# V and ones as weights from batch 2 on, with all attention steps at half slots: sparse attention beside a bilinear FFN

## Chip, cores, metric

One core of a Trainium2 chip. The metric is the device time of one execution in microseconds.

## The reference

```python
# q, k, v: (8, 8, 576, 64) f32, drawn * 0.1
scores = q @ k.T / 8                      # per batch and head, 576 x 576
local   = (0 <= i - j) & (i - j < 32)     # heads 0 to 3
strided = (0 <= i - j) & (j % 32 == i % 32)   # heads 4 to 7
attn = softmax(where(mask, scores, -1e9)); x = attn @ v
x -> (4608 tokens, 512 channels)
out = ((x @ w_a) * (x @ w_b)) @ w_out     # 512 -> 1536 -> 512
```

## The kernel before

The FFN runs over nine tiles of 512 tokens. A tile has 16 slots: 12 a/b slots (two groups of four matmuls, 1.73 us together) and four y slots (12 matmuls, 2.59 us). Attention steps of the next batch are put between the slots, since a tile needs the tokens of up to two batches. A batch has 8 S steps (scores, exp, mask), 8 V steps (probabilities times V, with a column of ones that gives the sums, then a reciprocal and a multiplication) and 4 X steps: TensorE (PE) transposes that bring the normalised output, tokens on partitions, to the channels-on-partitions form that the FFN reads, and a ScalarE copy. From batch 2 on, q and k are transposed by VectorE in 32x32 blocks ("D steps") and then moved to their places (`kT`, `qz`) by transfers that SyncE issues. The code is cut to the parts that matter.

```python
VW = 80
...
def step_D(b, z, nm, part):                   # z: 0 local heads, 1 strided
    nc.vector.transpose(t..., src...)         # 32x32 blocks
    if last:                                  # of k, or of q
        for nm, c in {"k": (("k", 0),), "q": (("q", 0), ("k", 1), ("q", 1))}[nm]:
            ...  nc.sync.dma_start(out=qz_buf[b % 2][j][z][...], in_=t[...])
...
def V_p(b, u):                                # from batch 2 on
    o = psum4["o"].tile([128, 2, 512], F32, tag="o", name="o")     # one buffer, two banks
    ...
    nc.tensor.matmul(of[:, j, i, :65], lhsT=p[:M, j, i*n:i*n+128], rhs=vt[..., 0:65], ...)
def V_r(b, u): nc.vector.reciprocal(rc, sums)
def V_n(b, u): nc.vector.tensor_mul(xn[...], o, rc broadcast)
def X_p(b, c): ... nc.tensor.transpose(tv[:, g, :], xn[:, g], ident)
def X_e(b, c): nc.scalar.copy(xT[:, c, S*b:S*(b+1)], tp)
...
open_psum(ctx, mm=3, tp=1, o=1)               # and "st", one buffer of two banks for scores
...
gs = {2: (13, 13, 14, 14, 15, 15, 16, 16, 17, 17), ...}    # slots of the ten D steps
for i, (fn, t, j) in enumerate(slots):
    fn(t, j, ...)                             # the FFN's work of the slot
    for f in at.get(i, ()): f()               # loads, D steps
    run(...)                                  # attention steps, whole slots
```

The softmax here doesn't subtract the row's maximum and nothing guards it: scores larger than these inputs give would overflow.

Of the kernel before, what the change touches and what calls it, by code (L numbers as in the profile page):

```python
# [7 lines left out]
F32 = mybir.dt.float32  # L8
BF16 = mybir.dt.bfloat16
I16 = mybir.dt.int16  # L10
ALU = mybir.AluOpType
ACT = mybir.ActivationFunctionType
ENG = mybir.EngineType

FIRST_D = 2
# [6 lines left out]
LW = 96  # L22
PAD = 32
PW = 344
VW = 80
WCH = (0, 2, 5, 8, 10, 12)


# [1 line left out]
def kernel(  # L30
# [66 lines left out]
    def consts(i):  # L97
# [7 lines left out]
        if i == 0:  # L105
            nc.vector.memset(vl_buf[0][:PAD, 0, 0:D], 0.0)

    spare = qz_buf[0][0][0][:, 0]

    def zero_qz(i, eng, parts=((0, 0), (0, 1), (1, 0), (1, 1))):  # L110
# [56 lines left out]
    def load_qk(b, strided, heads=range(HL), names="kq"):  # L167
        for nm in names:
            src = {"k": k, "q": q}[nm]
            if b < FIRST_D:  # L170
                n, R, h0 = (NP, RS, HL) if strided else (96, RL, 0)
                if (b, nm, strided) not in nats:
                    nats[b, nm, strided] = nat.tile([n, HL, R, D], BF16, tag=f"{nm}{R}", name=f"{nm}{R}", bufs=2)
                t = nats[b, nm, strided]
                hs = slice(heads[0], heads[-1] + 1)
                nc.gpsimd.dma_start(out=t[:, hs], in_=src[b, h0:h0 + HL].rearrange("h (p r) d -> p h r d", r=R)[:, hs])  # L176
            elif strided:

                t = nat_s[nm]
                n = 32 if b == FIRST_D else YS  # L180
                for h in heads:
                    nc.gpsimd.dma_start(  # L182
                        out=t[32 * h:32 * h + n],
                        in_=bass.AP(tensor=src.tensor, offset=(b * H + HL + h) * S * D,
                                    ap=[[RS * D, n], [YS * RS * D, 3], [1, RS * D]]))
            else:
                if 0 in heads:
                    nats[b, nm, strided] = nat.tile([128, NY, D], BF16, tag=f"{nm}l", name=f"{nm}l")
                t = nats[b, nm, strided]
                for h in heads:  # L190
                    nc.gpsimd.dma_start(out=t[32 * h:32 * h + 32],  # L191
                                        in_=src[b, h].rearrange("(i y) d -> y i d", y=32))
            nats[b, nm, strided] = t
# [122 lines left out]
    def unit(u):  # L316

        c, half = u // 2, u % 2
        return (c, half, 128, LW, 3) if c < 2 else (c, half, NP, NP, 4)
# [44 lines left out]
    def V_p(b, u):  # L364
        c, half, M, n, G = unit(u)
        p = ps.pop((b, u))
        if b == 0:

            o = psum4["o"].tile([128, 512], F32, tag="o", name="o")
            if c < 2:  # L370
                of = o[:, :2 * G * (D + 1)].rearrange("p (j g e) -> p j g e", j=2, e=D + 1)
                sm = of[:, :, :, D:]
            else:
                of = o.rearrange("p (j g e) -> p j g e", j=2, e=D)
                sm = psum4["sum"].tile([128, 2, 4, 1], F32, tag="sum", name="sum")
        else:
            o = psum4["o"].tile([128, 2, 512], F32, tag="o", name="o")
            of = o[:, :, :G * (D + 1)].rearrange("p j (g e) -> p j g e", e=D + 1)
            sm = of[:, :, :, D:]
        for i in range(G):  # L380
            for j in range(2):
                if c < 2:
                    vt = vl_buf[b % 2][:, (2 * c + j) * 6 + 3 * half + i, 0:D + 1]
                elif b == 0:
                    r = 2 * i + j
                    vt = nats[0, "v", c - 2][:NP, half, r * D:(r + 1) * D]
                elif b < FIRST_D:
                    vt = vs_buf[b % 2][:, 2 * (c - 2) + half, 2 * i + j, 0:D + 1]
                else:
                    vt = vs_buf[b % 2][:, 2 * (c - 2) + j, 4 * half + i, 0:D + 1]  # L390
                w = vt.shape[1]
                pt = p[:M, j, i * n:i * n + 128]
                nc.tensor.matmul(of[:, j, i, :w], lhsT=pt, rhs=vt, start=True, stop=True)  # L393
                if b == 0 and c >= 2:
                    nc.tensor.matmul(sm[:, j, i], lhsT=pt, rhs=vl_buf[0][:M, 0, D:D + 1], start=True, stop=True)
        held[b, "o", u] = of[:n, :, :, :D], sm[:n]
# [7 lines left out]
    def V_n(b, u):  # L404
        c, half, M, n, G = unit(u)
        ov, _ = held.pop((b, "o", u))
        rc = held.pop((b, "rc", u))
        if (b, c // 2) not in xn:
            xn[b, c // 2] = sb.tile([n, S // n, 4, D], BF16, tag=f"xn{n}", name=f"xn{n}", bufs=1)
        x = xn[b, c // 2][:, :, 2 * (c % 2):2 * (c % 2) + 2, :]  # L410
        if c < 2 or b >= FIRST_D:
            dst = x[:, G * half:G * half + G].rearrange("p g j d -> p j g d")
        else:
            dst = x[:, :, half, :].rearrange("p (g j) d -> p j g d", j=2)
        nc.vector.tensor_mul(dst, ov, rc[:n, :, :G].unsqueeze(3).to_broadcast([n, 2, G, D]))  # L415

    def step_V(b, u):
        V_p(b, u)
        V_r(b, u)
        V_n(b, u)  # L420

    def X_p(b, c):
        x = xn[b, c // 2][:, :, 2 * (c % 2):2 * (c % 2) + 2, :]
# [22 lines left out]
    def step_X(b, c):  # L446
# [12 lines left out]
        F1b F1c""".split()  # L459


    SEQ_T = {4: "Tk2", 5: "Tk3", 6: "Tq2", 7: "S4 Tq3", 8: "V4 S5", 9: "V5 S6 Tk0", 10: "V6 S7 Tq0",
             11: "V7 S0 X2", 11.5: "Tk1 S1", 12: "Tq1", 12.5: "X3 S2 V0", 13: "S3 V1", 13.5: "V2", 14: "V3 X0", 14.5: "X1"}
    DENSE = (("S0",), ("S1",), ("V0", "S2"), ("V1", "S3"), ("V2", "X0", "S4"), ("V3", "S5"), ("V4", "X1", "S6"),
             ("V5", "S7"), ("V6", "X2"), ("V7",), ("X3",))
    SEQ = (("S0",), ("S1",), ("V0",), ("S2",), ("V1",), ("S3", "X0"), ("V2",), ("S4",), ("V3",), ("S5", "X1"),
           ("V4",), ("S6",), ("V5",), ("S7", "X2"), ("V6",), ("V7",), ("X3",))
    FN = {"Tk": step_Tk, "Tq": step_Tq, "S": step_S, "V": step_V, "X": step_X}

    def run(b, slot):  # L470
        for s in slot:
            FN[s[:-1]](b, int(s[-1]))
# [1 line left out]

    pfs = {}

    def ab_mm(t, f, ab, kks):
        for w, ps_ in zip((wa_sb, wb_sb), ab):
            for kk in kks:
                nc.tensor.matmul(ps_, lhsT=w[:, kk, 128 * f:128 * (f + 1)], rhs=xT[:, kk, TTOK * t:TTOK * (t + 1)],  # L480
                                 start=(kk == 0), stop=(kk == KD - 1))

    def ffn_ab(t, f, ab=None):
        if f == 0:
            pfs[t] = fsb.tile([128, FD, TTOK], BF16, tag="pf", name="pf", bufs=1)
        pf = pfs[t]
        if ab is None:
            ab = [psum4["mm"].tile([128, TTOK], F32, tag="mm", name="mm") for _ in range(2)]
            ab_mm(t, f, ab, range(KD))
        a_sb = fsb.tile([128, TTOK], F32, tag="a_sb", name="a_sb")  # L490
        nc.scalar.copy(a_sb, ab[0])  # L491
        nc.vector.tensor_mul(pf[:, f, :], a_sb, ab[1])  # L492
        return pf[:1, f, :1]
# [21 lines left out]
    with tc.manual_schedule(engines={ENG.PE, ENG.SP, ENG.Pool, ENG.DVE, ENG.Activation}):  # L515
# [70 lines left out]
        slots = []  # L586
        for t in range(NT):
            slots += [(ffn_ab, t, f) for f in range(FD)] + [(ffn_y, t, j) for j in range(4)]
        todo = [(b, {2: 20}.get(b, 16 * (b - 1) - 2), list({2: DENSE}.get(b, SEQ)))
                for b in range(2, B)]  # L590
        at = {}

        def do(i, fn, *args):
            at.setdefault(i, []).append(lambda: fn(*args))

        for b in range(FIRST_D, B):
# [4 lines left out]
            else:  # L601
# [2 lines left out]
                    do(g0 + h + (6 if b == FIRST_D + 1 else 2), load_qk, b, True, (h,))  # L604
                    do(g0 + h + 10, load_vs, b, (h,))
                do(g0 + (10 if b == FIRST_D + 1 else 7), load_vl, b)
            gs = {2: (13, 13, 14, 14, 15, 15, 16, 16, 17, 17), 3: (8, 9, 10, 11, 12, 13, 14, 15, 16, 17)}.get(b) or (
                3, 5, 7, 9, 11, 12, 13, 14, 15, 17)
            for (z, nm, part), g in zip(((0, "k", 0), (0, "k", 1), (0, "q", 0), (0, "q", 1), (1, "k", 0), (1, "k", 1),
                                         (1, "k", 2), (1, "q", 0), (1, "q", 1), (1, "q", 2)), gs):  # L610
# [3 lines left out]
            do(6 + h, spread_vs, 1, h, nc.scalar.copy)  # L614
        do(1, zero_qz, 1, nc.vector, ((1, 1),))
        do(4, zero_qz, 1, nc.vector, ((1, 0),))
        for i, jz in ((2, (0, 0)), (3, (1, 0)), (12, (0, 1)), (12, (1, 1))):
            do(i, zero_qz, 0, nc.vector, (jz,))
        do(17, rezero, 1)
        for i, (fn, t, j) in enumerate(slots):  # L620
            if fn is ffn_y:
                done = fn(t, j, lambda: run(1, SEQ_T.get(i - 0.5, "").split()) if t == 0 else None)
            else:
                done = fn(t, j, first.get(j) if t == 0 else None)
            if i > 13 and i in at:

                nc.gpsimd.tensor_copy(pace, done)  # L627
            for f in at.get(i, ()):
                f()
            run(1, SEQ_T.get(i, "").split())  # L630
            for b, g0, seq in todo:
                if seq and i >= g0:
                    run(b, seq.pop(0))
# [1 line left out]
_INS = ['q', 'k', 'v', 'moe_w_a', 'moe_w_b', 'moe_w_out']  # L635
_OUTS = [((4608, 512), 'float32')]
# [25 lines left out]
```

## Time and profile before

| | before |
|---|---|
| time, median of 4 | 345.4 us (344.6 to 345.9) |
| TensorE busy | 98% |
| tile 0 / tile 1 / tiles 2 to 5 each / tile 6 / tile 7 | 42.83 / 36.61 / 35.90 / 35.40 / 31.08 us |
| gaps on TensorE in tiles 0 / 1 / 2 | 3.95 / 0.20 / none |

A tile is counted from the start of its first FFN matmul to that of the next tile. A gap is the distance between the starts of two neighbouring matmuls less the time in which the first streams its columns (columns / 2.4 GHz + 2.5 ns, which fits this trace: 216 ns for 512 columns, 43 for 96); this shows waits that the modelled ends of matmuls hide. The page and the views of this kernel are read in the prediction. One more view matters later, the one of the tile `qz01l`, a part of the transposed q, between 58 and 68 us: instruction, count, shortest, median and longest issue in ns, first and last start; then the time from issue to landing.

```profile
L299 SPq DMA_DIRECT2D qz01l<-tq x4: 539/590/1216, 60.3 to 66.8; - x4
...
DMA to landing us min/median/max: 2.6/4.1/6.4
```

Batch 2's first S step needs the first two of these and the first two of `qz00l`. The last of the four was issued at 62.18 us and landed 5.1 us later, at 67.3. TensorE came to the step at 70.35 us, with 3.1 us in hand:

```profile
70.35 0.21 PE L337 MATMUL st<-qz00l,kT0l 128*128 128x96 bf16 x1
```

### The profile page before, as it was taken

The numbers are of one execution on the slowest core, as the hardware profiler recorded it, in microseconds if no ns is written. First come the engines' busy times: TensorE is split into PE (matmuls) and PEld (weight loads), VectorE is DVE, ScalarE is ACT, GpSimd is POOL, SyncE is SP. The second block draws the span as 40 slices with busy tenths as digits, with TensorE's granted clock in tenths as the row PEclk, the third lists the DMA queues.
The fourth block names the chain that finished last, engine by engine and source line by source line (L and its number), as shares of the span: only waits on it lengthen the run. The fifth ranks groups of instructions, "written<-read, shape, count | busy, mean of one in ns | idle before, by whom it ended". The sixth has DMA issues, their size and how long they took to land.

```text
span 343.2 us, 7085 instructions
## 1 busy us (share of the span) xinstructions
PE 335.8 (98%) x2688; PEld 176.9 (52%) x2688; DVE 198.5 (58%) x400; ACT 152.8 (45%) x259; POOL 131.9 (38%) x243
## 2 busy tenths in 40 slices
PE   8999998999999999999999999999999999999995
PEld 6754554455555555555555555555555544444444
DVE  6865677669747764777377746774666323303331
ACT  5654864456255534544454435543454243223311
POOL 8944539596556334743375246533000000000000
PEclk9999999999999999999999999999999999999999
DMA  9999999996999879969996999788220110020002
GB/s 158 146 202 199 202 174 197 175 146 94 124 192 128 88 112 152 111 90 104 151 122 104 90 158 112 131 69 145 69 54 2 63 61 0 3 92 31 0 32 92
DMA packets 102243, 37.57 MB, mean 109 GB/s; under 512 B 77633, under 2 KB 97729, under 8 KB 102209
## 3 DMA queue, kind: packets, MB, share of 16 engines
q0 software_dynamic: 87760, 19.58, 62.3%
q1 hardware_dynamic: 14304, 17.47, 15.9%
q8 instruction: 21, 0.34, 0.4%
q14 instruction: 14, 0.11, 0.1%
q10 hardware_dynamic: 144, 0.07, 0.1%
HBM read 39.71 MB, written 9.44 MB: 143 GB/s over the span
## 4 chain that ended last, share of the span: by engine, by line
PE 81%; DMA 12%; POOL 4%; DVE 1%; issue 1%; ACT 0%; POOLq 0%; ACTq 0%
PE mm L480 48%; PE mm L502 24%; DMA vl<-in_v_dram 4%; PE st L337 4%; DMA k<-in_k_dram 3%; PE o L393 3%; DMA wa_sb<-in_moe_w_a_dram 3%; PE tp L428 2%; DMA out_dram<-y_sb 1%; DMA natk<-in_k_dram 1%; POOL q L176 1%; POOL vl L203 1%; POOL k L176 1%; POOL wa_sb L224 0%; POOL wb_sb L224 0%
## 5 line engine op out<-in xcount | busy, mean ns | idle before, releaser
L492 DVE TENSOR_TENSOR pf<-a_sb,mm 128x512 bf16<-128x512 f32 x106 | 72.8, 687 | 81.7 <-PE mm L480 77.9
L480 PE MATMUL mm<-xT,wa_sb 128*128 128x512 bf16 x424 | 108.9, 379 | 0.0
L480 PE MATMUL mm<-xT,wb_sb 128*128 128x512 bf16 x424 | 108.8, 379 | 0.0
L502 PE MATMUL mm<-wo_sb,pf 128*128 128x512 bf16 (+2 forms) x456 | 98.9, 368 | 0.0
L491 ACT COPY a_sb<-mm 128x512 f32<-128x512 f32 x106 | 62.0, 585 | 82.3 <-PE mm L480 80.8
L480 PEld LDWEIGHTS <-wb_sb 128*128 128x128 bf16 x432 | 42.2, 98 | 51.2 <-issue 0.4
L502 PEld LDWEIGHTS <-pf 128*128 128x128 bf16 x456 | 41.6, 98 | 42.6
L480 PEld LDWEIGHTS <-wa_sb 128*128 128x128 bf16 x432 | 37.4, 98 | 33.4
L345 ACT ACTIVATE p<-st 128x576 bf16<-128x576 f32 (+1 forms) x64 | 41.7, 651 | 25.9 <-PE st L337 25.8
L508 ACT COPY y_sb<-mm 128x512 f32<-128x512 f32 (+2 forms) x35 | 19.9, 570 | 70.6 <-PE mm L502 48.8
L415 DVE TENSOR_TENSOR xn<-o,rc 96x384 bf16<-96x384 f32 (+1 forms) x64 | 39.6, 620 | 2.1
L393 PEld LDWEIGHTS <-p 72*128 72x128 bf16 (+1 forms) x448 | 22.0, 97 | 16.5 <-DVE xn L415 3.5
L355 DVE TENSOR_TENSOR p<-p,mask_l 128x576 int16<-128x576 int16 x32 | 14.2, 443 | 24.6 <-ACT p L345 24.6
L627 POOL CAST pace<-pf 1x1 f32<-1x1 bf16 x51 | 8.9, 175 | 41.0 <-DVE pf L492 29.0
L215 POOL DMA_DIRECT2D vs<-in_v_dram x24 | 19.6, 817 | 10.6 <-issue 8.9
L444 ACT COPY xT<-tp 128x576 bf16<-128x576 bf16 x31 | 19.6, 634 | 3.3 <-PE tp L428 3.1
L401 DVE RECIPROCAL rc<-o 96x6 f32<-96x6 f32 (+1 forms) x60 | 11.3, 189 | 16.1 <-PE o L393 15.8
L191 POOL DMA_DIRECT2D kl<-in_k_dram x24 | 16.0, 665 | 7.4 <-issue 5.5
L191 POOL DMA_DIRECT2D ql<-in_q_dram x24 | 16.0, 666 | 5.8 <-DMA wo_sb<-in_moe_w_out_dram 3.7
L182 POOL DMA_DIRECT2D natk<-in_k_dram x24 | 14.6, 610 | 6.3 <-issue 6.3
L627 POOL COPY pace<-y_sb 1x1 f32<-1x1 f32 x22 | 3.8, 174 | 29.5 <-ACT y_sb L508 29.5
L182 POOL DMA_DIRECT2D natq<-in_q_dram x24 | 14.6, 608 | 0.0
(106 smaller groups left out, 283.1 us busy)
## 6 DMA issues: line engine op xcount, KB each, us to landing
out_dram<-y_sb SPq DMA_DIRECT2D x35, 256.0 KB, 2.1
vl<-in_v_dram POOLq DMA_DIRECT2D x7, 384.0 KB, 6.6
kl<-in_k_dram POOLq DMA_DIRECT2D x24, 72.0 KB, 3.1
ql<-in_q_dram POOLq DMA_DIRECT2D x24, 72.0 KB, 3.2
vs<-in_v_dram POOLq DMA_DIRECT2D x24, 72.0 KB, 3.7
wo_sb<-in_moe_w_out_dram POOLq DMA_DIRECT2D x4, 384.0 KB, 11.6
natk<-in_k_dram POOLq DMA_DIRECT2D x20, 72.0 KB, 3.1
natq<-in_q_dram POOLq DMA_DIRECT2D x20, 72.0 KB, 3.3
```

The lines of the kernel that those rows point to most:

```text
L182: nc.gpsimd.dma_start(out=t[32 * h:32 * h + n], in_=bass.AP(tensor=src.tensor, offset=(b * H + HL + h) * S * D, ap=[[RS * D, n], [YS * RS ...
L191: nc.gpsimd.dma_start(out=t[32 * h:32 * h + 32], in_=src[b, h].rearrange("(i y) d -> y i d", y=32))
L215: nc.gpsimd.dma_start(out=vs_buf[b % 2][:, h, :, 0:D], in_=v[b, HL + h].rearrange("(p r) d -> p r d", r=RS))
L345: nc.scalar.activation(p[:M, :, :W], st[:M, :, :W], ACT.Exp, scale=scale)
L393: nc.tensor.matmul(of[:, j, i, :w], lhsT=pt, rhs=vt, start=True, stop=True)
L415: nc.vector.tensor_mul(dst, ov, rc[:n, :, :G].unsqueeze(3).to_broadcast([n, 2, G, D]))
L444: nc.scalar.copy(dst, tv)
L480: nc.tensor.matmul(ps_, lhsT=w[:, kk, 128 * f:128 * (f + 1)], rhs=xT[:, kk, TTOK * t:TTOK * (t + 1)], start=(kk == 0), stop=(kk == KD - 1))
L491: nc.scalar.copy(a_sb, ab[0])
L492: nc.vector.tensor_mul(pf[:, f, :], a_sb, ab[1])
L502: nc.tensor.matmul(y, lhsT=pf[:, f, 128 * j:128 * (j + 1)], rhs=wo_sb[:, f, c0:c0 + n], start=(f == 0), stop=(f == FD - 1))
L508: (nc.scalar.copy if act else nc.vector.tensor_copy)(y_sb, y)
```

## The change

V with 64 columns of ones becomes the stationary operand and the probabilities the moving one. The output then has channels on partitions 0 to 63 and the sums, repeated, on 64 to 127. So no transpose is needed: ScalarE makes 1/sum as exp(-ln(sum)), VectorE multiplies twice and writes xT itself, for the strided heads with a stride. The price is 128-wide V buffers, filled with ones by GpSimd. All attention steps get positions in half slots, batch 2's D steps move (most of them one slot later), and the first group of a tile takes the channel that is made last at its end. The diff is shortened.

```diff
-VW = 80
+VW = 128
+def fill_v(t):
+    nc.gpsimd.memset(t[..., D:], 1.0)
...
+def step_VT(b, u):                                   # b >= 2
+    nc.tensor.matmul(o[:, j, i*n:(i+1)*n], lhsT=vt, rhs=p[:M, j, i*n:(i+1)*n], ...)
+    nc.scalar.activation(r, sums, ACT.Ln)            # o[64:], 64 x 576
+    nc.scalar.activation(r, r, ACT.Exp, scale=-1.0)
+    for j in range(2):
+        nc.vector.tensor_mul(xT[64*j:64*j+64, c, ...], o[:64, j, :W], r[:, j])
...
-SEQ_T, DENSE, SEQ = ...                              # whole slots, X steps in them
+STEPS = {1: {5: "Tk2", 5.5: "Tk3", ... 15: "X1"},
+         2: {20: "S0", 20.5: "S1", 21.5: "V0", 22: "S2", ... 30.5: "V7"}}
+LATER = {-2: "S0", -1: "S1", 0: "V0", 1: "S2", 2: "V1", ... 12: "V6", 13.5: "V7"}
...
+late = 1 if t == 1 else 3                            # first group of a tile
+ab_mm(t, f, ab, [kk for kk in range(KD) if kk != late], last=-1)
+ab_mm(t, f, ab, [late], first=-1, last=late)
...
-gs = {2: (13, 13, 14, 14, 15, 15, 16, 16, 17, 17), ...
+gs = {2: (14, 14, 14, 15, 16, 16, 17, 17, 18, 18), ...
+for i, t in ((0, vl_buf[0]), (0, vs_buf[0]), (18, vl_buf[1]), (19, vs_buf[1])):
+    do(i, fill_v, t)
```

Cut: one buffer in place of two for batch 0's and 1's q and k, one shared buffer for `xn` and `r`, other slots for some memsets, and the D steps now stand behind the attention steps of their slot in the queues.

More of the change, by code (lines that the diff above doesn't have):

```diff
@@ L106, in consts @@
             nc.vector.memset(vl_buf[0][:PAD, 0, 0:D], 0.0)
+    def fill_v(t):
+        nc.gpsimd.memset(t[:, :, :, D:] if len(t.shape) == 4 else t[:, :, D:], 1.0)
     spare = qz_buf[0][0][0][:, 0]
@@ L172, in load_qk @@
                 if (b, nm, strided) not in nats:
-                    nats[b, nm, strided] = nat.tile([n, HL, R, D], BF16, tag=f"{nm}{R}", name=f"{nm}{R}", bufs=2)
+                    nats[b, nm, strided] = nat.tile([n, HL, R, D], BF16, tag=f"{nm}{R}", name=f"{nm}{R}", bufs=1)
                 t = nats[b, nm, strided]
@@ L386, in V_p @@
                     vt = nats[0, "v", c - 2][:NP, half, r * D:(r + 1) * D]
-                elif b < FIRST_D:
+                else:
                     vt = vs_buf[b % 2][:, 2 * (c - 2) + half, 2 * i + j, 0:D + 1]
-                else:
-                    vt = vs_buf[b % 2][:, 2 * (c - 2) + j, 4 * half + i, 0:D + 1]
                 w = vt.shape[1]
@@ L408, in V_n @@
         if (b, c // 2) not in xn:
-            xn[b, c // 2] = sb.tile([n, S // n, 4, D], BF16, tag=f"xn{n}", name=f"xn{n}", bufs=1)
+            x = sb.tile([128, RS * 4 * D], BF16, tag="xr", name="xr", bufs=2)
+            xn[b, c // 2] = x[:n, :S // n * 4 * D].rearrange("p (g h d) -> p g h d", h=4, d=D)
         x = xn[b, c // 2][:, :, 2 * (c % 2):2 * (c % 2) + 2, :]
@@ L417, in step_V @@
     def step_V(b, u):
+        if b >= FIRST_D:
+            step_VT(b, u)
+            return
         V_p(b, u)
@@ L420, in step_V @@
         V_n(b, u)
+    def step_VT(b, u):
+        c, half, M, n, G = unit(u)
+        p = ps.pop((b, u))
+        o = psum4["o"].tile([128, 2, 512], F32, tag="o", name="o")
+        for i in range(G):
+            for j in range(2):
+                if c < 2:
+                    vt = vl_buf[b % 2][:, (2 * c + j) * 6 + 3 * half + i]
+                else:
+                    vt = vs_buf[b % 2][:, 2 * (c - 2) + j, 4 * half + i]
+                nc.tensor.matmul(o[:, j, i * n:(i + 1) * n], lhsT=vt, rhs=p[:M, j, i * n:(i + 1) * n], start=True, stop=True)
+        r = sb.tile([128, RS * 4 * D], BF16, tag="xr", name="xr", bufs=2)[:64, :4 * W].bitcast(F32)
+        r = r.rearrange("p (j w) -> p j w", j=2)
+        if c < 2:
+            sums = o[64:, :, :W]
+        else:
+            sums, r = (t.rearrange(e, p=NP) for t, e in ((o[64:, :, :W], "d j (g p) -> d j p g"), (r, "d j (p g) -> d j p g")))
+        nc.scalar.activation(r, sums, ACT.Ln)
+        nc.scalar.activation(r, r, ACT.Exp, scale=-1.0)
+        for j in range(2):
+            dst = xT[64 * j:64 * j + 64, c, S * b:S * (b + 1)]
+            if c < 2:
+                nc.vector.tensor_mul(dst[:, W * half:W * (half + 1)], o[:64, j, :W], r[:, j])
+            else:
+                nc.vector.tensor_mul(dst.rearrange("d (p r) -> d p r", r=RS)[:, :, G * half:G * (half + 1)],
+                                     o[:64, j, :W].rearrange("d (g p) -> d p g", p=NP), r[:, j])
     def X_p(b, c):
@@ L459 @@
         F1b F1c""".split()
-    SEQ_T = {4: "Tk2", 5: "Tk3", 6: "Tq2", 7: "S4 Tq3", 8: "V4 S5", 9: "V5 S6 Tk0", 10: "V6 S7 Tq0",
-             11: "V7 S0 X2", 11.5: "Tk1 S1", 12: "Tq1", 12.5: "X3 S2 V0", 13: "S3 V1", 13.5: "V2", 14: "V3 X0", 14.5: "X1"}
-    DENSE = (("S0",), ("S1",), ("V0", "S2"), ("V1", "S3"), ("V2", "X0", "S4"), ("V3", "S5"), ("V4", "X1", "S6"),
-             ("V5", "S7"), ("V6", "X2"), ("V7",), ("X3",))
-    SEQ = (("S0",), ("S1",), ("V0",), ("S2",), ("V1",), ("S3", "X0"), ("V2",), ("S4",), ("V3",), ("S5", "X1"),
-           ("V4",), ("S6",), ("V5",), ("S7", "X2"), ("V6",), ("V7",), ("X3",))
+    STEPS = {1: {5: "Tk2", 5.5: "Tk3", 6: "Tq2", 7: "S4", 7.5: "Tq3", 8: "S5", 8.5: "V4", 9: "S6 Tk0", 9.5: "V5", 10: "S7 Tq0",
+                 10.5: "V6", 11: "S0 Tk1", 11.5: "V7", 12: "Tq1 S1", 12.5: "V0 X2", 13: "S2", 13.5: "V1 X3 S3", 14: "V2",
+                 14.5: "V3 X0", 15: "X1"},
+             2: {20: "S0", 20.5: "S1", 21.5: "V0", 22: "S2", 23: "V1", 23.5: "S3", 24.5: "V2", 25: "S4", 26: "V3", 26.5: "S5",
+                 27.5: "V4", 28: "S6", 28.5: "V5", 29: "S7", 29.5: "V6", 30.5: "V7"}}
+    LATER = {-2: "S0", -1: "S1", 0: "V0", 1: "S2", 2: "V1", 3: "S3", 4: "V2", 5: "S4", 6: "V3", 7: "S5", 8: "V4", 9: "S6",
+             10: "V5", 11: "S7", 12: "V6", 13.5: "V7"}
     FN = {"Tk": step_Tk, "Tq": step_Tq, "S": step_S, "V": step_V, "X": step_X}
@@ L475, with ab_mm, ffn_ab @@
     pfs = {}
-    def ab_mm(t, f, ab, kks):
+    def ab_mm(t, f, ab, kks, mid=None, first=0, last=KD - 1):
         for w, ps_ in zip((wa_sb, wb_sb), ab):
+            if mid and ps_ is ab[1]:
+                mid()
             for kk in kks:
                 nc.tensor.matmul(ps_, lhsT=w[:, kk, 128 * f:128 * (f + 1)], rhs=xT[:, kk, TTOK * t:TTOK * (t + 1)],
-                                 start=(kk == 0), stop=(kk == KD - 1))
-    def ffn_ab(t, f, ab=None):
+                                 start=(kk == first), stop=(kk == last))
+    def ffn_ab(t, f, mid, ab=None):
         if f == 0:
@@ L488, in ffn_ab @@
             ab = [psum4["mm"].tile([128, TTOK], F32, tag="mm", name="mm") for _ in range(2)]
-            ab_mm(t, f, ab, range(KD))
+            if f == 0:
+                late = 1 if t == 1 else 3
+                ab_mm(t, f, ab, [kk for kk in range(KD) if kk != late], last=-1)
+                ab_mm(t, f, ab, [late], first=-1, last=late)
+            else:
+                ab_mm(t, f, ab, range(KD), mid)
         a_sb = fsb.tile([128, TTOK], F32, tag="a_sb", name="a_sb")
@@ L588, with take @@
             slots += [(ffn_ab, t, f) for f in range(FD)] + [(ffn_y, t, j) for j in range(4)]
-        todo = [(b, {2: 20}.get(b, 16 * (b - 1) - 2), list({2: DENSE}.get(b, SEQ)))
-                for b in range(2, B)]
+        steps = {}
+        for b in range(1, B):
+            for pos, names in (STEPS.get(b) or {16 * (b - 1) + x: n for x, n in LATER.items()}).items():
+                steps.setdefault(pos, []).append((b, names.split()))
+        def take(pos):
+            for b, names in steps.get(pos, ()):
+                run(b, names)
         at = {}
@@ L606 @@
                 do(g0 + (10 if b == FIRST_D + 1 else 7), load_vl, b)
-            gs = {2: (13, 13, 14, 14, 15, 15, 16, 16, 17, 17), 3: (8, 9, 10, 11, 12, 13, 14, 15, 16, 17)}.get(b) or (
+            gs = {2: (14, 14, 14, 15, 16, 16, 17, 17, 18, 18), 3: (8, 9, 10, 11, 12, 13, 14, 15, 16, 17)}.get(b) or (
                 3, 5, 7, 9, 11, 12, 13, 14, 15, 17)
@@ L616 @@
         do(4, zero_qz, 1, nc.vector, ((1, 0),))
-        for i, jz in ((2, (0, 0)), (3, (1, 0)), (12, (0, 1)), (12, (1, 1))):
+        for i, jz in ((2, (0, 0)), (3, (1, 0)), (0, (0, 1)), (5, (1, 1))):
             do(i, zero_qz, 0, nc.vector, (jz,))
         do(17, rezero, 1)
+        for i, t in ((0, vl_buf[0]), (0, vs_buf[0]), (18, vl_buf[1]), (19, vs_buf[1])):
+            do(i, fill_v, t)
         for i, (fn, t, j) in enumerate(slots):
-            if fn is ffn_y:
-                done = fn(t, j, lambda: run(1, SEQ_T.get(i - 0.5, "").split()) if t == 0 else None)
-            else:
-                done = fn(t, j, first.get(j) if t == 0 else None)
+            mid = lambda: take(i - 0.5)
+            done = fn(t, j, mid) if fn is ffn_y else fn(t, j, mid, first.get(j) if t == 0 else None)
             if i > 13 and i in at:
                 nc.gpsimd.tensor_copy(pace, done)
+            take(i)
             for f in at.get(i, ()):
                 f()
-            run(1, SEQ_T.get(i, "").split())
-            for b, g0, seq in todo:
-                if seq and i >= g0:
-                    run(b, seq.pop(0))
 _INS = ['q', 'k', 'v', 'moe_w_a', 'moe_w_b', 'moe_w_out']
```

## The prediction

> **What bounds the kernel now.** I read the page's busy shares first, then the windows table cut at the starts of the token tiles, then the chain that ended last, then the timeline of TensorE, then its waits.
>
> ```profile
> PE 335.8 (98%) x2688; PEld 176.9 (52%) x2688; DVE 198.5 (58%) x400; ACT 152.8 (45%) x259; POOL 131.9 (38%) x243
> ...
> core 0: us, PE busy (x) PEld busy (x) DVE busy (x) ACT busy (x) POOL busy (x), PEclk, DMA share, GB/s
> 98.49:134.40 35.91, 35.91 (x286) 18.89 (x284) 24.18 (x47) 16.31 (x29) 17.44 (x35) 1.00 0.95 124
> 134.40:170.30 35.90, 35.90 (x285) 18.87 (x284) 23.76 (x46) 16.30 (x29) 17.33 (x35) 1.00 0.91 118
> 242.10:277.50 35.40, 35.40 (x274) 18.36 (x272) 17.95 (x36) 15.58 (x27) 0.35 (x2) 1.00 0.14 45
> 61.88:98.49 36.61, 36.58 (x297) 19.22 (x296) 25.27 (x49) 17.33 (x30) 22.98 (x41) 1.00 1.13 145
> 18.89:61.72 42.83, 40.25 (x380) 21.19 (x377) 28.15 (x57) 24.30 (x42) 24.08 (x34) 1.00 1.48 193
> ```
>
> TensorE (PE) is the bound, at the full clock. From tile 2 on (98.49 us) it has no idle at all, and one tile with one batch of attention beside it takes 35.90 us. Tile 1 (61.88 to 98.49) is nearly full. Tile 0, with batch 1 beside it, has idle: 42.83 us long, 40.25 busy. In the chain that ended last, the two last tiles, without attention, give the price of pure FFN:
>
> ```profile
> 277.50 20.72 PE mm L480 x96
> 298.22 10.36 PE mm L502 x48
> ```
>
> That is 31.08 us for 144 matmuls, 216 ns each. So in a full tile attention takes 35.90 - 31.08 = 4.82 us of TensorE. The timeline says of what:
>
> ```profile
> 102.22 1.03 PE L480 MATMUL mm<-xT,wa_sb 128*128 128x512 bf16 x4
> 103.08 1.03 PE L480 MATMUL mm<-xT,wb_sb 128*128 128x512 bf16 x4
> 103.95 0.35 PE L393 MATMUL o<-vl,p 128*128 128x65 bf16 x6
> 104.13 1.02 PE L480 MATMUL mm<-xT,wa_sb 128*128 128x512 bf16 x4
> ...
> 106.11 0.42 PE L428 MATMUL tp<-ident,xn 96*128 96x96 bf16 x6
> 106.37 0.81 PE L480 MATMUL mm<-xT,wa_sb 128*128 128x512 bf16 x3
> ```
>
> The printed durations overlap; what counts is start to start. A V step (probabilities times V) of a local head pair is 104.13 - 103.95 = 0.18 us (6 x 65 columns), an X step (transposing the normalised output) 106.37 - 106.11 = 0.26 us. Read the same way, a strided V step (8 x 65) is 0.24, a strided X step (8 x 72) 0.26 to 0.27, an S step (scores) 0.25 to 0.26 for 6 x 96 columns and 0.25 for 8 x 72. Per batch: V 4 x 0.18 + 4 x 0.24 = 1.68, X 2 x 0.26 + 2 x 0.265 = 1.05, S 8 x 0.255 = 2.04; sum 4.77 of the 4.82. Nothing of it waits.
>
> In tile 0 TensorE's own waits are:
>
> ```profile
> PE o L393 <- DVE xn L415: 1.2, 2, 0.7
> PE tp L250 <- DMA k<-in_k_dram: 0.7, 1, 0.7
> PE o L393 <- DVE p L355: 0.5, 1, 0.5
> ```
>
> With the pipe's drain around each, the start-to-start gaps that I find on its timeline between 18.89 and 61.72 us are 0.3 (21.4), 0.8 (28.2), 0.7 (39.4), 0.3 in small ones, 0.25 (51.4), 0.65 (53.9) and 0.9 (56.0): some 3.9 us.
>
> **What the Trainium skill says.** (1) "TensorE: Matmul & The Clock Gate", the section on the 56 ns gap: back to back, a warm matmul takes N / 2.4 GHz plus about 2.5 ns. The trace agrees: 215.8 against 216 ns at N = 512, 30 against 29.6 at 65, 43 against 42.5 at 96. So swapping weights and moving operand costs by columns moved alone. (2) "ScalarE: Activation LUTs", What ACT_TABLE_LOAD costs and the part before it: one element per cycle whatever the function, and Ln and Exp share a table set. The trace has Exp on 576 columns at 651 ns and a copy of 576 at 634 and one table load in all; the Ln is in no run yet. (3) "VectorE: DVE Perf Modes", the errata section: an fp32 tensor_tensor takes (N + 151)/0.96 ns. Here 512 columns take 687 ns and 384 take 553, which is (N + 147)/0.96. (4) "Perfetto Trace Analysis", Identifying the Most-Contended Engine: matmul busy time misleads because matmuls are pipelined. Here too: the busy sum over the groups is above the span, and only starts give costs.
>
> **The change part by part.**
>
> *Removed from TensorE, batches 2 to 7:* all X steps, 1.05 us a batch. *Added:* V steps now stream 96 or 72 queries instead of 65 columns, so they cost what S steps of the same shape cost: 4 x (0.255 - 0.18) + 4 x (0.25 - 0.24) = 0.34 us. Net -0.71 us a batch.
>
> *ScalarE, per batch:* gone are four copies xT<-tp of 634 ns (2.5 us), new are 8 x (Ln 0.65 + Exp 0.67) = 10.6 us (an estimate from the 576-column rows). 16.3 + 8.1 = 24.4 of about 35.2 us: 69%, not a bound.
> *VectorE, per batch:* gone are 8 reciprocals (181 and 197 ns) and 8 multiplications (553 and 687), 6.5 us; new are 16 of 288 columns at (288 + 147)/0.96 = 453 ns, 7.2 us. 23.8 + 0.7 = 24.5 of 35.2: 70%.
>
> *The new chain from V to V.* There is one two-bank output buffer; the next V may start once both multiplications have read it. From V's end, by hand: 0.2 drain, Ln to 0.85, Exp to 1.55, multiplications to about 2.6. From batch 3 on V stands every second slot, which gives 2 x 1.73 + 0.25 = 3.7 us in the a/b slots and 3.9 in the y slots: at least 1 us of slack. The FFN's own three PSUM buffers: the multiplication pf of the slot after V comes behind V's two on VectorE, ends about 3.5 after V, and its buffer is wanted at 4.3. So tiles 2 to 6 stay without idle: 5 x 0.71 = **-3.6 us**.
>
> *Tile 1 (batch 2).* Pure price after: 31.08 + 4.77 - 0.71 + 0.51 for batch 3's first two S steps = 35.65, against 36.6. But V stands every 1.5 slots there, or 2.85 us from V's end to the next V, against the chain's 2.6. In 1.5 slots (3.1 us) ScalarE has 0.88 + 0.65 + 1.32 = 2.85 us of work, and VectorE 1.03 + 0.44 + 0.91 = 2.4 plus up to 1.1 of the 32x32 transposes. I take back 0.4 us for new waits: **-0.6 us**.
>
> *Tile 0 (batch 1).* Nothing is cheaper; only the waits can go. Tk2 a slot later meets its k already landed (-0.8). V half a slot after the S before it, with the mask done, takes 0.7 and the small gaps. But transfers then bind:
>
> ```profile
> 48.01 0.66 POOL L191 DMA_DIRECT2D ql<-in_q_dram x1 [0.96 <-DMA wo_sb<-in_moe_w_out_dram]
> 50.79 0.66 POOL L191 DMA_DIRECT2D ql<-in_q_dram x1 [2.12 <-DMA vl<-in_v_dram]
> ```
>
> GpSimd issues each load as an earlier one lands, so these lines date landings: the last part of wo_sb at 48.0, batch 1's V at 50.5 to 50.8. Without waits TensorE would want that wo_sb part, in the second half of the first y slot, at about 46.7; it ended that half at 49.67 before and can't end it before 48.65. So of 3.9 us only about 1 is won up to there. Later, batch 2's transposes (three of 0.77 in one go at slot 14) stand on VectorE between V2's and V3's multiplication, and X1 needs V3's: I work out 1 us of waiting there. Start of tile 1 then: about 60.2 instead of 61.7: **-1.5 us**. Halving the q and k buffers costs nothing (their readers of batch 0 are done by 13 us, the reload is issued at 15.4), nor do the fills with ones on GpSimd delay a load that is wanted at once.
>
> *"Last-made channels last"* takes no work away: it gives the last channel 6 x 0.216 = 1.3 us more. It guards the starts of tiles 1 and 2; elsewhere there was no gap to take.
>
> Sum: -3.6 - 0.6 - 1.5 = -5.7 us; 345.26 - 5.7 = **339.6 us**, 1.6% less.
>
> **Rivals.**
> 1. *The new normalisation binds.* If Ln, Exp or the strided multiplications take over 0.3 us longer each than worked out, the V-to-V wait replaces the transposes. For: one output buffer, a chain over two engines, densest in tile 1. Against: copies out of PSUM read in permuted order (the strided X steps) are no slower than straight ones here, and 1 us of slack. It would give 342 to 345.
> 2. *Tile 0 gives everything back.* Against the waits of the old order, the loads at 48 and 50.5 us and the transposes on VectorE: tile 1 starts at 61.5 still, about 341. For: DMA is at its busiest there (1.48 in the window). Against: the waits at 53.9 and 56.0 come after the loads and are VectorE's order alone.
> 3. *Tile 0 and 1 lose all their idle* (landings come earlier than I date them, transposes fit in): -2.5 and -0.95, about 338.2, just over 2%.
>
> **Range and chances.** The -3.6 us is counted and I trust it to 0.3; tile 0 lies between -0.3 and -2.7, tile 1 between 0 and -0.95. That gives 337.9 to 341.6. Over 2% faster needs under 338.4, so nearly every wait gone: 0.17. Slower by 2% needs a stall of 2 us in every tile, which no row speaks for: 0.02. Within 2%: 0.81.
>
> **What would show it.** Right: tiles 2 to 6 35.2 us each with TensorE full; a V step of 0.25 us; no xT<-tp copies after batch 1; Ln and Exp near 0.66 us; multiplications near 0.45; tile 1 starting near 60.2. Wrong: waits of V's matmuls for the multiplications in tiles 2 to 6 (rival 1), or a wait for wo_sb or for X1's input that keeps tile 1's start at 61.5 (rival 2), or a start under 59.5 (rival 3).

## More of the kernel before

`kT` holds the transposed k; `qz` holds the transposed q, in buffers such as `qz00l` and `qz01l` (batch parity, head of a pair, local or strided).

## The result

The changed kernel takes 344.0 us (343.3 to 344.4, 4 runs), before 345.4. The ratio is 0.996 (95% interval 0.9935 to 0.9984). Ratios here are the mean time of one kernel's fast runs over that of the other's of the same rounds, so not quite the ratio of the medians quoted. It is faster, by 0.4%, not by the 1.6% foretold, and above the 337.9 to 341.6 us that the prediction gave.

The page and the windows table of the changed kernel, cut at its tile starts (0 and 1, then 2, 3, 5 and 6):

```profile
PE 333.1 (98%) x2520; PEld 173.7 (51%) x2520; DVE 205.1 (60%) x400; ACT 203.9 (60%) x331; POOL 140.4 (41%) x247
...
18.51:59.36 40.85, 40.05 (x380) 21.62 (x377) 26.35 (x55) 24.46 (x42) 23.45 (x31) 1.00 1.41 189
59.36:98.69 39.33, 36.74 (x272) 18.65 (x271) 26.72 (x49) 24.95 (x42) 29.98 (x49) 1.00 1.36 143
98.69:134.61 35.92, 35.76 (x260) 18.29 (x258) 26.65 (x49) 24.93 (x42) 18.07 (x35) 1.00 0.91 127
134.61:170.07 35.46, 35.38 (x261) 18.27 (x259) 24.79 (x46) 24.92 (x41) 17.94 (x35) 1.00 0.91 119
205.52:240.97 35.45, 35.41 (x261) 18.29 (x259) 24.80 (x46) 24.92 (x41) 16.58 (x33) 1.00 0.92 119
240.97:275.67 34.70, 34.70 (x248) 17.69 (x246) 19.24 (x37) 24.35 (x39) 0.44 (x2) 1.00 0.14 46
```

The second row is the result: tile 1 became longer by 2.7 us, and TensorE idles in it.

| part of the span | before | after | difference | predicted |
|---|---|---|---|---|
| start-up, to tile 0 | 18.89 | 18.51 | -0.4 | 0 |
| tile 0 | 42.83 | 40.85 | -2.0 | -1.5 |
| tile 1 | 36.61 | 39.33 | **+2.7** | -0.6 |
| tiles 2 to 6 | 179.01 | 176.98 | -2.0 | -3.6 |
| tile 7 to the end | 65.86 | 65.83 | 0 | 0 |
| span | 343.2 | 341.5 | -1.7 | -5.7 |

TensorE's waits in tile 1 (engine, line, what it waited for: us in total, times, longest). Before, the same view of this stretch is empty.

```profile
PE st L340 <- DMA qz11l<-tq: 1.2, 1, 1.2
PE st L340 <- DMA qz00l<-tq: 0.7, 1, 0.7
PE st L340 <- DMA qz01l<-tq: 0.5, 1, 0.5
```

The first S steps of batches 2 and 3 on TensorE's timeline, with the FFN matmuls ahead of the first:

```profile
67.13 1.03 PE L518 MATMUL mm<-xT,wb_sb 128*128 128x512 bf16 x4
68.83 0.20 PE L340 MATMUL st<-qz00l,kT0l 128*128 128x96 bf16 x1 [0.67 <-DMA qz00l<-tq]
69.52 0.22 PE L340 MATMUL st<-qz01l,kT0l 128*128 128x96 bf16 x1 [0.49 <-DMA qz01l<-tq]
...
95.13 0.20 PE L340 MATMUL st<-qz10l,kT1l 128*128 128x96 bf16 x1 [1.24 <-DMA qz11l<-tq]
```

The four matmuls from 67.13 us stream for 0.86 us, so TensorE was ready for S at 68.0. These are S steps waiting for transposed q, not V steps waiting for the new normalisation. By starts the gaps are 0.84 and 0.65 us at 68 us (batch 2's first S step), 1.41 and 0.20 at 93.7 (batch 3's), and two of 0.24 ahead of FFN groups: 3.57 in all against 0.20 before. That accounts for the tile: 36.61 - 0.20 - 0.71 + 3.57 = 39.27.

The rows of the new normalisation, from the page (count, busy us, mean ns, idle before):

```profile
L447 ACT ACTIVATE xr<-o 64x576 f32<-64x576 f32 x48 | 31.1, 647 | 23.5 <-PE o L438 23.3
L454 DVE TENSOR_TENSOR xT<-o,xr 64x288 bf16<-64x288 f32 x48 | 21.6, 450 | 33.1 <-ACT xr L448 32.8
L448 ACT ACTIVATE xr<-xr 64x576 f32<-64x576 f32 x48 | 32.8, 682 | 1.5
L452 DVE TENSOR_TENSOR xT<-o,xr 64x288 bf16<-64x288 f32 x48 | 21.6, 450 | 16.9 <-ACT xr L448 16.4
```

They cost what was worked out (0.65, 0.67 and 453 ns), and the strided writes (L454) no more than the straight ones (L452).

What happened to q: GpSimd's timeline of the changed kernel, and of the kernel before at the same place,

```profile
50.06 0.66 POOL L194 DMA_DIRECT2D ql<-in_q_dram  x1 [1.80 <-DMA vl<-in_v_dram]
50.72 1.40 POOL L109 MEMSET vl<- 128x1536 bf16 x1
52.03 1.83 POOL L109 MEMSET vs<- 72x2048 bf16 x1
53.78 2.22 POOL L185 DMA_DIRECT2D natk<-in_k_dram  x4
```

```profile
51.44 2.21 POOL L182 DMA_DIRECT2D natk<-in_k_dram  x4
```

and the view of `qz01l` after, answering to the one shown of before:

```profile
L302 SPq DMA_DIRECT2D qz01l<-tq x4: 507/561/592, 60.5 to 67.4; - x4
...
DMA to landing us min/median/max: 5.7/6.9/7.6
```

The two fills take 3.2 us of GpSimd's queue just ahead of the loads of the strided q, k and V. Those are issued later and run beside the transfers of q, which now take 6.9 us to land in place of 4.1 (medians). The four parts that S needs were issued at the same time as before, within 0.4 us (first issue of `qz` 59.87 us, before 59.67), though tile 0 ended 2.4 us earlier, so S came at 68.0 us, not 70.35. That the issue did not move forward with tile 0 has to do with the D steps, which the change puts a slot later. Three causes for one wait, then: q landed later, S came sooner, and the issue stayed where it was. The experiments try to pull them apart.

### The profile page after: what moved, and what is told of

Its sections match the earlier page's. It is cut to its first block, busy times and chain, and to the rows that moved or that the text cites. A ratio compares the mean times of both kernels' runs of the same rounds, so it can differ in the third digit from the quotient of the medians.

```text
span 341.5 us, 6887 instructions
## 1 busy us (share of the span) xinstructions
PE 333.1 (98%) x2520; PEld 173.7 (51%) x2520; DVE 205.1 (60%) x400; ACT 203.9 (60%) x331; POOL 140.4 (41%) x247
## 4 chain that ended last, share of the span: by engine, by line
PE 70%; DMA 17%; SPq 3%; DVE 3%; ACT 3%; POOL 2%; issue 2%; DVEq 0%; ACTq 0%
PE mm L518 41%; PE mm L546 20%; DMA vl<-in_v_dram 4%; PE o L438 3%; PE st L340 3%; DMA k<-in_k_dram 3%; DMA wa_sb<-in_moe_w_a_dram 3%; SPq L302 2%; DMA qz01l<-tq 2%; PE misc L153 2%; DMA out_dram<-y_sb 1%; DMA qz01s<-tq 1%; ACT xr L447 1%; DMA qz11s<-tq 1%; DVE tq L283 1%
## 5 line engine op out<-in xcount | busy, mean ns | idle before, releaser
L518 PE MATMUL mm<-xT,wb_sb 128*128 128x512 bf16 x424 | 110.1, 379 | 0.3
L518 PE MATMUL mm<-xT,wa_sb 128*128 128x512 bf16 x424 | 110.2, 379 | 0.1
L536 DVE TENSOR_TENSOR pf<-a_sb,mm 128x512 bf16<-128x512 f32 x106 | 71.9, 678 | 48.3 <-PE mm L518 25.5
L518 PEld LDWEIGHTS <-wb_sb 128*128 128x128 bf16 x432 | 41.7, 98 | 49.5 <-issue 1.3
L518 PEld LDWEIGHTS <-wa_sb 128*128 128x128 bf16 x432 | 38.1, 98 | 34.2 <-issue 0.2
L447 ACT ACTIVATE xr<-o 64x576 f32<-64x576 f32 x48 | 31.1, 647 | 23.5 <-PE o L438 23.3
L454 DVE TENSOR_TENSOR xT<-o,xr 64x288 bf16<-64x288 f32 x48 | 21.6, 450 | 33.1 <-ACT xr L448 32.8
L448 ACT ACTIVATE xr<-xr 64x576 f32<-64x576 f32 x48 | 32.8, 682 | 1.5
L452 DVE TENSOR_TENSOR xT<-o,xr 64x288 bf16<-64x288 f32 x48 | 21.6, 450 | 16.9 <-ACT xr L448 16.4
L678 POOL CAST pace<-pf 1x1 f32<-1x1 bf16 x51 | 11.6, 227 | 41.5 <-DVE pf L536 41.3
```

The costliest lines, as they stand in the source:

```text
L447: nc.scalar.activation(r, sums, ACT.Ln)
L448: nc.scalar.activation(r, r, ACT.Exp, scale=-1.0)
L452: nc.vector.tensor_mul(dst[:, W * half:W * (half + 1)], o[:64, j, :W], r[:, j])
L454: nc.vector.tensor_mul(dst.rearrange("d (p r) -> d p r", r=RS)[:, :, G * half:G * (half + 1)], o[:64, j, :W].rearrange("d (g p) -> d p g", ...
L518: nc.tensor.matmul(ps_, lhsT=w[:, kk, 128 * f:128 * (f + 1)], rhs=xT[:, kk, TTOK * t:TTOK * (t + 1)], start=(kk == first), stop=(kk == last))
L536: nc.vector.tensor_mul(pf[:, f, :], a_sb, ab[1])
```

## The experiments

Tile times and gaps are from each run's own profile. One execution of e1 (346.8 us) and one of e7 (345.5) were slow; the medians include them (without them 343.2 and 340.5), the ratios do not. Single executions scatter by 1 to 4 us around the median, most visibly in the start-up: tile 0 begins at 18.5 to 20.0 us, and in one profile at 22.1 (e6_all_three, where the granted clock was 0.91 over the first 18.5 us and 0.50 from 20 to 24 us, so into tile 0). So I compare tile lengths within profiles, and times by medians and ratios. In the profiles of after_again and e5 to e8 the record of tile 2's first matmul is missing (two are shown where the changed kernel's profile has three), so that the tile seems to start 0.22 us late; the table is corrected for it.

| run | median us | ratio to before (95%) | tile 0 | tile 1 | tiles 2 to 6 |
|---|---|---|---|---|---|
| e1_fill_early | 343.5 | 0.995 (0.989 to 1.001) | 40.95 | 37.80 | 176.80 |
| e2_old_slots | 342.5 | 0.992 (0.986 to 0.997) | 40.40 | 39.09 | 178.24 |
| e3_v_alone | 347.1 | 1.004 (0.999 to 1.009) | 42.58 | 39.08 | 178.37 |
| e4_sched_alone | 344.9 | 0.997 (0.992 to 1.002) | 41.58 | 37.16 | 178.99 |
| after_again | 344.9 | 0.996 (0.992 to 1.000) | 41.62 | 39.75 | 177.53 |
| e5_s0_later | 342.7 | 0.990 (0.988 to 0.993) | 40.86 | 38.27 | 177.16 |
| e6_all_three | 341.3 | 0.987 (0.984 to 0.990) | 41.59 | 36.97 | 177.23 |
| e7_no_q_b23 | 340.6 | 0.985 (0.982 to 0.988) | 40.69 | 36.23 | 176.79 |
| e8_four_banks | 340.7 | 0.984 (0.979 to 0.989) | 41.53 | 36.49 | 176.65 |
| e9_best | 339.4 | 0.981 (0.976 to 0.985) | 40.85 | 36.08 | 176.26 |

### e1: the fills out of the way

```diff
-for g, fn, *a in ((0, load_qk, b, False), (1, load_qk, b, True), ...
+for g, fn, *a in ((0, fill_v, vl_buf[0]), (0, load_qk, b, False, range(HL), "k"),
+                  (0, fill_v, vs_buf[0]), (0, load_qk, b, False, range(HL), "q"), (1, load_qk, b, True), ...
-for i, t in ((0, vl_buf[0]), (0, vs_buf[0]), (18, vl_buf[1]), (19, vs_buf[1])):
+for i, t in ((18, vl_buf[1]), (19, vs_buf[1])):
```

> The fills of the two V buffers with ones on GpSimd are moved from behind batch 2's first q and k loads to between them, where GpSimd waits for earlier loads to land anyway. Theory A (the fills hold back the loads behind them by 3.2 us, these then collide with the transfers of the transposed q, which take 7.6 us to land where they took about 4): the landing of qz comes back to 4 to 5 us, the two gaps of 0.84 and 0.65 us ahead of batch 2's first S step at 68 us vanish, tile 1 (39.3 us) takes about 37.8, the whole about 342.5 us. Rival B (tile 0 became shorter, so S comes 2.4 us sooner to transfers that land when they always did): the gaps stay over 1 us together and the time stays within 0.4 us of the changed kernel's 344.0.

Landing of `qz01l` fell from 6.9 to 5.1 us (medians; the 7.6 above is the slowest part), the gaps at batch 2's first S step from 1.49 to 0.60, and batch 3's from 1.61 to 0.96. Tile 1 is 37.80, the number of theory A, but only in part for its reason: 0.65 of the 1.53 us came at batch 3, of which A says nothing. The median time fell short (343.5, not 342.5), with fast runs from 341.6 to 343.9: of the time nothing is shown here, of the mechanism some 60% of the wait at batch 2. The remaining 0.6 us needs another cause.

### e2: batch 2's transposes in their old slots

```diff
-gs = {2: (14, 14, 14, 15, 16, 16, 17, 17, 18, 18),
+gs = {2: (13, 13, 14, 14, 15, 15, 16, 16, 17, 17),
```

> The changed kernel with batch 2's VectorE transposes in their old slots (13 to 17 in place of 14 to 18). Rival C (the later slots make q late for batch 2's first S step): the gaps of 1.5 us at 68 us vanish and the time falls by 1 us or more, to about 343. Theory A (late and colliding loads): landing of qz still 6 us or more, the gaps shrink by half at most, and tile 0 loses up to 0.9 us to V steps waiting behind the transposes: 343.7 to 344.7.

Landing stayed slow (6.5 us), as A says, but the gap at batch 2's first S step vanished, as C says, and the time is some 1.5 us under the changed kernel's (the intervals of the two ratios overlap). So neither has it alone: the wait is issue plus landing against TensorE's arrival. Here the sooner issue removed it. The loss of tile 0 that I expected did not come. In this run's profile, which fell on its slowest execution (345.25 us), batch 3's first S step waited 2.4 us instead, and S steps on the strided heads 0.7 to 0.8 us in each of tiles 2 to 4: what is won ahead of one transfer is waited away at the next.

### e3: V as weights alone, in the old order

```diff
 # the kernel before, with VW = 128, fill_v, step_VT, the shared xr buffer, and
+if b >= FIRST_D and s[0] == "X": continue
```

> The kernel before with V and ones as weights alone: old order of steps (X steps of batches 2 to 7 dropped), no half slots, no late channel, fills as in the change. If the price of the steps is as I worked out, tiles 3 to 6 take 35.2 to 35.5 us in place of 35.9 and tile 0 42.8 as before. In tile 1 the old order has V in every slot, 2.2 us apart, against a chain of about 2.6: waits of V for its output buffer of 0.3 to 0.5 us at each of 6 steps, so tile 1 at 37.5 to 39. The whole 342 to 344. If instead the step has a hidden cost of its own, tiles 3 to 6 stay above 35.6 here too.

Slower than I expected, 347.1 us, and not shown to be faster or slower than before. TensorE's waits:

```profile
PE o L440 <- DVE xT L454: 1.8, 4, 0.5
PE o L440 <- DVE xT L456: 1.6, 7, 0.4
```

In tile 1, where the old order has a V in every slot, six V steps wait 0.32 to 0.68 us each for the one output buffer (3.3 us by starts), and once more, 0.36, in each of tiles 2 to 6. Tiles 2 to 5 take 35.82, above the 35.2 to 35.5 expected; less these gaps and one of 0.24 ahead of an FFN group it is 35.2, so the price of the steps was right. The longer chain of Ln, Exp and two multiplications is real, and the new positions are what hides it: without them no gain is shown.

### e4: the schedule alone, with the old V and X steps

```diff
-VW = 128
+VW = 80
 # step_V as before, no fills, X steps put back:
+23.5: "S3 X0", 26.5: "S5 X1", 29: "S7 X2", 31: "X3"      (batch 2; later batches likewise)
```

> The changed kernel's half slots, late channels and moved transposes with the old V and X steps and without the fills. Tile 0 as in the changed kernel (waits 2.0 us in place of 3.95). Theory A (the fills are what makes q late): no gap over 0.5 us ahead of batch 2's first S step, tile 1 about 36.9, tiles 2 to 6 35.9 as before, the whole about 343.2. Rival B (S merely comes too soon): gaps of 1 us or more there without any fill, the whole about 344.6.

Tile 0 gains 1.25 us here (the second half of the first y slot waited 0.9 us for wo_sb, as I had feared for the change), tiles 2 to 6 are as before, and no S step waits: q lands in 4.5 to 4.8 us (medians), and S comes at 69.1, 1.1 us later than in the changed kernel. That is for A, though it does not exclude B, since S came later too. The time is 344.9, above the 343.2 expected: by the ratio the schedule alone wins 1 us, and no gain at all lies inside the interval.

### The changed kernel once more

> The changed kernel once more, as the base of the other runs of this call on the same chip. Both theories: 0.996 of the kernel before within 0.003; the gaps ahead of S steps in tiles 1 and 2 in the profile again (batch 2's first S step about 1.5 us together, batch 3's about 1.6).

The ratio is the same, 0.9962. In this profile (an execution of 345.5 us) batch 2's first S step waited 2.4 us and batch 3's 1.2.

### e5: batch 3's first S step later

```diff
-{16 * (b - 1) + x: n for x, n in LATER.items()}
+{16 * (b - 1) + (-1.5 if (b, x) == (3, -2) else x): n for x, n in LATER.items()}
```

> The changed kernel with batch 3's first S step half a y slot later (behind V7 of batch 2 in place of ahead of the last y slot but one). Theory D (in tile 1 the transposed q of batches 2 and 3 land at times that TensorE does not set, so what TensorE saves ahead of them is waited away at the S step): the gap of 1.6 us there falls under 0.4, no work is delayed by it, the time falls by 1.0 to 1.6 us against the changed kernel, unless the next S steps of batch 3 on the strided heads then wait instead. Rival E (the S step is only the place where a slow normalisation chain shows): the gap moves along and the time stays.

The wait for q at batch 3 is gone, and the time fell by 0.6% of the kernel before, 2 us, against the changed kernel: theory D, though the two intervals overlap, and 2 us is more than the wait that went (batch 3's gaps were 1.2 to 1.6 us). A smaller wait took its place: the second S step, now close behind, waited 0.67 us for the one score buffer, whose Exp stands behind the Ln and Exp of V7 on ScalarE.

### e6: the three moves together

```diff
 # the edits of e1, e2 and e5
```

> Fills in GpSimd's waiting time, batch 2's transposes in their old slots, and batch 3's first S step half a slot later, together. Theory D: both gaps under 0.5 us, tile 1 36.0 to 36.6 us, the whole 1.5 to 3 us under the changed kernel, about 341.5. Rival E: no more than the 0.4 to 1.4 us that the first two moves gave alone.

341.3 us, 0.9% under the changed kernel. Both waits for q in tile 1 are gone; its 36.97 us are above the 36.0 to 36.6 expected, 0.71 of it the wait for the score buffer. This profile fell on the slowest execution, and its late start-up gave q more time; but e8, which holds the same moves and began tile 0 at 18.8 us, has no wait for q in tile 1 either.

### e7: no transposed q for batches 2 and 3

```diff
-for j in range(2):                      # in step_D, the transfers of q
+for j in range(2 if b > 3 else 0):
```

> Wrong result on purpose: the changed kernel without the transfers of the transposed q of batches 2 and 3 (S multiplies what lies there), so that no S step of these batches can wait for them; everything else stands. Theory D: all gaps ahead of S steps in tiles 1 and 2 are gone but for those on k, tile 1 takes 36.2 us or less and the time falls by 3 us or more against the changed kernel, to about 340.5. Rival E: waits for VectorE or ScalarE take their place and the time falls by less than 1.5 us.

This is no valid kernel. (The comparison with the reference passed all the same: with inputs of 0.1 a score is a sum of 64 products of about 0.01 divided by 8, so about 0.01, and softmax hardly depends on q.) The windows table, tiles 0 to 2:

```profile
19.12:59.81 40.69, 39.56 (x366) 21.45 (x372) 26.05 (x55) 24.25 (x42) 23.29 (x31) 1.00 1.40 190
59.81:96.26 36.45, 35.98 (x266) 18.80 (x271) 26.97 (x50) 25.05 (x43) 30.11 (x49) 1.00 1.38 135
```

No S step waits in tiles 1 and 2, tile 1 takes 36.23 (the 36.45 of the row less the 0.22 of the missing record), and the time is 340.6: 3.9 us (1.1%) under the changed kernel by the ratios, whose intervals do not meet. That is the settling run: with nothing changed but that S can't wait for q, most of the missing gain is there, as theory D has it, and rival E falls. (With the q transfers gone the other transfers have more room, too, so the run bounds both causes together.)

### e8: four PSUM banks for the FFN

```diff
-ab = [psum4["mm"].tile([128, TTOK], F32, tag="mm", name="mm") for _ in range(2)]
+ab = [bank(TTOK) for _ in range(2)]     # every fourth from tile 1 on is the transposes' bank, free by then
-y = psum4["mm"].tile([128, n], F32, tag="mm", name="mm")
+y = bank(n)
```

> On top of the three moves together (341.3 us): from tile 1 on the FFN's outputs take turns over four PSUM banks in place of three (the transposes' bank is free by then). If the gaps of 0.24 us ahead of an a or b group (one or two a tile) are buffers that free late because the copy a_sb stands behind Ln and Exp on ScalarE, they vanish: tiles 4 and 5 35.2 in place of 35.45, the whole 1 to 1.3 us less, about 340.2. If they have another cause (Ln and Exp late, V's buffer), they stay.

The gaps of 0.24 us ahead of FFN groups are gone and tile 5 takes 35.22 in place of 35.45. So they were buffers: the copy `a_sb` frees one and stands behind Ln and Exp on ScalarE. Tile 4 kept its 35.45, by a gap of 0.22 ahead of an S step of the strided heads. In the changed kernel's profile the order is to be seen: Exp ended at 74.4 us, the copy `a_sb` behind it at 75.06, and the group that had the gap began at 75.10. By ratios the gain over e6 (of another call) is 0.3% and lies inside the intervals.

### e9: and the strided heads' waits for q

```diff
+{30.5: "S0", 32: "V0 S1"} if b == 3 else ...              # S1 of batch 3 after V0
-3: (8, 9, 10, 11, 12, 13, 14, 15, 16, 17), later (3, 5, 7, 9, 11, 12, 13, 14, 15, 17)
+3: (8, 9, 10, 11, 12, 13, 13, 14, 15, 16), later (3, 5, 7, 9, 11, 12, 12, 13, 14, 15)
```

> On top of that: batch 3's second S step after tile 2's first slot (in e6 it waited 0.7 us for the one score buffer, behind Exp of V7's normalisation on ScalarE), and the last transposes of q for the strided heads one slot sooner from batch 3 on (S waits of 0.35 to 0.6 us in tiles 2 to 4). Theory D: these gaps fall under 0.2 us, tile 1 36.3 or less, tiles 2 to 5 35.2 to 35.3, the whole 339.2 to 340, 0.983 to 0.985 of the kernel before. Rival: VectorE, with the transposes sooner, delays the multiplications, and V waits instead: no gain over e8.

```profile
59.89:95.97 36.08, 35.60 (x261) 18.40 (x264) 26.29 (x48) 24.77 (x41) 27.25 (x46) 1.00 1.39 142
...
132.10:167.10 35.00, 34.79 (x252) 18.10 (x256) 24.75 (x46) 24.70 (x41) 17.84 (x35) 1.00 0.93 120
167.10:202.31 35.21, 34.94 (x255) 18.19 (x258) 24.75 (x46) 24.91 (x41) 17.94 (x35) 1.00 0.94 120
```

339.4 us (339.2 to 340.4), 0.981 of the kernel before: faster than both kernels, and valid. Whether by more than 2% the interval (0.976 to 0.985) leaves open; it is wide since some runs of the kernel before in that call took 348 to 349 us, at a granted clock of 0.983 to 0.989. Tiles 3 to 5 take 35.2 us, the price without waits (the record of tile 3's first matmul is missing, so its row is 0.22 us short). One S step of batch 3 counts in tile 2 here, 0.25 us. Not every wait is gone: batch 2's first S step has gaps of 0.16 and 0.38 us, the longer one ended by `qz01l`, and batch 3's second S step one of 0.45, ended by an Exp that frees the score buffer.

## Why the prediction was wrong

*Prices: right.* A V step at the price of an S step and no X step, -0.71 us a batch: tile 6, with no gap, went from 35.40 to 34.70. Ln, Exp and the multiplications took what their rows foretold, and V never waited for them in tiles 1 to 6 of the changed kernel. Rival 1 (the normalisation binds) did not happen in that form; e3 shows that it happens in the old order.

*Tile 0: right in kind, -2.0 for -1.5.* The two waits that I named, for wo_sb and for X1's input, came at 0.25 and 0.55 us in this profile where I had worked out about 1 each; wo_sb's came between nothing and 1.1 us in others. Rival 2 (everything given back in tile 0) falls; rival 3's -2.5 is not reached.

*Tile 1: the step that failed.* It is the sum "35.65, against 36.6 ... I take back 0.4 us for new waits: -0.6 us". The mechanism that I priced, V's output buffer and the load of ScalarE and VectorE, cost no V a wait. I did not ask what the S steps wait for. Their q comes over a path of its own (load, VectorE transposes, SyncE's issues, a transfer of 3 to 7 us) that did not move forward with TensorE; before, it was done 3.1 us ahead of S for batch 2 and 0.3 us ahead for batch 3, and showed as no wait in any view. TensorE came 2.4 us sooner, the transposes stood a slot later, the transfers took longer, and the path became the bound: 3.1 us by starts at two S steps. e7 takes this path away and gets 3.9 us back; by the ratios e5 gets about 2 of them back with a move alone, e6 about 3, and e9, with other waits gone too, about 5. With it, one sentence of mine was wrong outright: that the fills do not "delay a load that is wanted at once". They delayed loads by 3.2 us; these were not wanted at once, but they then ran beside transfers that were.

*Tiles 2 to 6: mis-sized, -2.0 for -3.6.* The term 5 x 0.71 held; "so tiles 2 to 6 stay without idle" did not. Gaps of 0.65, 0.24, 0.20 and 0.21 us stand in tiles 2 to 5: 0.42 and 0.24 are waits for the strided heads' q (e9 removes them), the rest FFN groups waiting for a buffer (e8 removes that of tile 5). I had checked the buffer that the multiplication `pf` frees, not the one that the copy `a_sb` frees behind Ln and Exp. Some 0.2 us of the difference is in no gap that I can name.

*The order of channels.* At the tile starts there is no gap in the profile of the changed kernel but X1's 0.55. I did not undo this part alone, so its own worth stays open.

*How much each cause did at batch 2.* The fourth of the parts that the first S step needs, in us from the start of tile 0:

| profile | issued | took to land | landed | TensorE ready for S | in hand |
|---|---|---|---|---|---|
| before | 43.3 | 5.1 | 48.4 | 51.5 | 3.1 |
| changed | 43.3 | 7.6 | 51.0 | 49.5 | -1.5 |
| e1 (fills early) | 44.3 | 5.9 | 50.2 | 49.6 | -0.6 |
| e2 (old D slots) | 41.4 | 6.5 | 47.8 | 49.5 | 1.7 |
| e4 (no fills, old V and X) | 44.8 | 5.0 | 49.8 | 50.2 | 0.5 |
| e9 | 42.0 | 8.1 | 50.0 | 49.5 | -0.5 |

The slower landing took 2.5 us and the earlier arrival 2.0; the 3.1 us that were in hand would have borne either alone (an estimate from the first two rows), and with the D steps in their old slots no wait was left (e2). That the fills are what slows the landing stays open: e1 says yes for a part, but in e9, with the fills early, the part took 8.1 us. That q is the cause, e7 shows.

Three readings in the prediction are to be put right, none of which bears on its sum. Its windows from 61.88 us on are cut 0.16 us late (tile 1 starts at 61.72, tile 2 at 98.33). That Ln and Exp share a table set stands in the page's next section, "Table sets: the hidden batching unit". The lower end of its range should be 337.7 us by its own terms.

## What to carry to other kernels

Where one engine is full, a cheaper step moves every later step of that engine forward; so list, for each kind of step that follows, when its inputs land and with how much slack, also those that show no wait now. A path with little slack (load, transpose, transfer) turned the gain into a wait at the place where it is read, and in e2 and e5 part of the wait only went to the next reader. An instruction added to a queue that issues loads delayed the loads behind it, by 3.2 us here; place it where that queue waits anyway.

## What the Trainium skill lacked or had wrong

- "DMA: Bandwidth & Descriptors", the anatomy of one DMA, puts a transfer that GpSimd issues at about 2.0 us plus bytes / 436 GB/s. By that, an estimate, a 72 KB load takes 2.2 us; the loads of `natk` took 3.1 (median, before). For the 36 KB of a `qz` part, which SyncE issues and the formula does not cover, it would give 2.1 us; these took 2.6 to 6.4 us before and 5.7 to 7.6 in the changed kernel (the windows table's DMA share between 60 and 70 us: 1.73, then 2.03). The page has no figure for how long a whole transfer takes to land beside others.
- "TensorE: Matmul & The Clock Gate", Back-to-back issue gap, gives about 131 ns a matmul at 512 columns and 81 at 128 for a stream of weight loads and matmuls. Such streams ran here at 216 ns for 512 columns and 43 for 96, which is the formula that the page calls isolated.
- No page that I found prices a GpSimd memset: 128 x 1536 bf16 took 1.40 us, 72 x 2048 took 1.83.
- "ScalarE: Activation LUTs", What ACT_TABLE_LOAD costs, has for immediates 186 ns + 0.833 ns per element, so 666 ns for 576. The Ln out of PSUM took 647 and the Exp out of SBUF 682, so the formula is 3% high for the one and 2% low for the other.
